# Linear attention with two MoE layers: the attention stage in a fixed order on three engines, set conversion steps, own PSUM banks, a Heron step

## The chip, the cores and the metric

The kernel runs on one core of a Trainium2 chip. The metric is the device time of one execution in microseconds (us). TensorE (PE in the profile) multiplies, VectorE (DVE) and ScalarE (ACT) work elementwise, SyncE (SP) issues the loads and stores. A kernel before and a kernel after the change compute the same function of the same inputs.

## The reference, cut to what matters

```python
batch, n_heads, seq, head_dim = (4, 8, 576, 64)          # n_tokens 2304, d_model 512
kv = np.einsum('bhsd,bhse->bhde', k, v)
out = np.einsum('bhsd,bhde->bhse', q, kv)
rms = np.sqrt(np.mean(out * out, axis=-1, keepdims=True) + 1e-06)
x = (out / rms * g_norm)                                 # then heads side by side: 2304 x 512
h = x @ w_in                                             # 512 -> 2048
g = h * np.clip(h + 3.0, 0.0, 6.0) / 6.0
x = g @ w_out                                            # 2048 -> 512
p = domain_probs / (domain_probs.sum(-1, keepdims=True) + 1e-09)
for e in range(4):                                       # 512 -> 1024 -> 512
    h = np.maximum(x @ w1[e], 0.0)
    out += p[:, e:e + 1] * (h @ w2[e])
```

`moe_w_in` and `moe_w_out` arrive as 64-bit floats, `x` and everything else as 32-bit.

## The kernel before, in words

The work has three stages: attention, the first MoE, the second MoE. The change touches the first, and the order in which the second begins.

Attention works on eight half-batches (`NHB`), each four heads of one batch. For half-batch i, `att_load` issues the loads of q, k and v on SP, 576 KB each, into seven buffers taken in turn. `att_q` transposes q on PE (`pq`, the last of nine columns into `kvp`), and ScalarE copies it to `qT`. `att_kv` adds up k transposed times v on PE (`kvp`), and ScalarE copies the blocks to `kvbd`. `att_out` multiplies qT with kvbd on PE (`po`, three PSUM banks); ScalarE squares it into `xt` and VectorE reduces the squares to `ssq`. `att_rms` makes the reciprocal root from it, in small steps on 128 x 20 elements, and scales po into `xt`. `att_x` transposes the scaled tile on PE (`px`, three pieces), ScalarE writes the high part `xh` and VectorE the low part `xl` of what the MoE reads. The loop over i runs `att_q` and `att_kv` of i, `att_out` and `att_rms` of i - 1 and `att_x` of i - 2.

The first MoE takes 16 tiles of weights (`ftiles`) in groups (`UNITS1`), and for each group goes over five blocks of tokens (four of 512, one of 256). `ff_in` is the first product of one tile and one block: 12 matmuls into a `psa` bank, then two steps on ScalarE and two on VectorE that leave `gH` and `gL`. `ff_out` is the second product, 12 matmuls into four banks, three items (`LAG`) behind `ff_in`. At a group's end `ff_end` copies (first group, ScalarE) or adds (later groups, VectorE) the banks to `acc`. Some first products (`EARLY`, `fill`) run during the attention.

Each weight tile must be turned from 64-bit to two 32-bit parts: `convert` does it in two halves, each with three steps on ScalarE and seven on VectorE, over raw data that `load_raw` brings into three buffers. `conv(k)` runs k pieces of it in the attention, `pull` runs it during the MoE by a budget per item.

The program is recorded in the order of the code; a scheduler then decides the order on each engine, and places the waits. PSUM has eight banks: two in `psa` (q transposes, first products), five in `psb` and one in `psc` (all else).

Of the kernel before, what the change touches and what calls it, by code (L numbers as in the profile page):

```python
# [17 lines left out]
def kernel(  # L18
# [34 lines left out]
    UNITS1 = (2, 4, 4, 6)  # L53
# [7 lines left out]
    NA = NW - UNITS1[0]  # L61
    LAG = 3
    FMAX = 3.0e38
# [18 lines left out]
    psb = ctx.enter_context(tc.tile_pool(name="psb", bufs=5, space=bass.MemoryType.PSUM))  # L82
    psc = ctx.enter_context(tc.tile_pool(name="psc", bufs=1, space=bass.MemoryType.PSUM))
# [3 lines left out]
    def bank_b(shape, name):  # L87
        turn[0] += 1
        pool, tag = (psc, "c") if turn[0] % 6 == 0 else (psb, "b")
        return pool.tile(shape, F32, tag=tag, name=name)  # L90
# [4 lines left out]
    three = const.tile([P, 1], F32, name="three")  # L95
    gcol = const.tile([P, 1], F32, name="gcol")
# [13 lines left out]
    raw = {}  # L110

# [18 lines left out]
    def convert(n):  # L130

        u, f = ftiles[n]
        w = wp.tile([P, 2, 2, KD * P], F32R, tag=f"w{(NA + n) % NW}", name="w")
        W[u, f] = w

        for h in range(2):
# [9 lines left out]
                out=xf, in0=xf, scalar1=2.0 ** -15, scalar2=122880.0, op0=ALU.max, op1=ALU.min)  # L146
            nc.vector.tensor_scalar(
                out=x, in0=x, scalar1=5, scalar2=2,
                op0=ALU.logical_shift_left, op1=ALU.logical_shift_right)
            yield 670  # L150
            nc.vector.scalar_tensor_tensor(
                out=a, in0=hi, scalar=0xC0000000, in1=x, op0=ALU.bitwise_and, op1=ALU.bitwise_or)
            nc.vector.tensor_scalar(out=x, in0=a, scalar1=0xFF800000, scalar2=None, op0=ALU.bitwise_and)
            yield 940
            nc.vector.tensor_tensor(out=r, in0=r, in1=xf, op=ALU.mult)
            nc.vector.tensor_tensor(out=r, in0=r, in1=a.bitcast(F32), op=ALU.add)
            yield 1200
# [3 lines left out]
            load_raw()  # L161
            yield 600


# [38 lines left out]
    def att_q(i):  # L203
# [3 lines left out]
        qv = qTs.rearrange("p r (s j) -> p r s j", j=CJ)  # L207
        pq = [psa.tile([P, CB, CP], F32, tag="a", name="pq") for _ in range(NP)]
        t["kvp"] = kvp = [bank_b([P, 2, D], "kvp") for _ in range(NP)]
        for j in range(CJ):  # L210
            for x in range(2):
                for r in range(NP):
                    to = pq[r][half[x ^ r], j, :] if j < CB else kvp[r][half[x ^ r], 1, :]
                    nc.tensor.matmul(  # L214
                        to, lhsT=t["q"][half[x], r, j, :], rhs=ident[half[x], half[x]], start=True, stop=True)
        for r in range(NP):
            nc.scalar.activation(out=qv[:, r, :, :CB], in_=pq[r].rearrange("p j s -> p s j"), func=AF.Copy)  # L217
        for r in range(NP):
            nc.scalar.activation(out=qv[:, r, :, CB], in_=kvp[r][:, 1, :], func=AF.Copy)

    def att_kv(i):
# [4 lines left out]
        for j in range(CJ):  # L226
            for x in range(2):
                for r in range(NP):
                    nc.tensor.matmul(  # L229
                        kvp[r][half[x ^ r], 0, :], lhsT=t["k"][half[x], r, j, :], rhs=t["v"][half[x], r, j, :],  # L230
                        start=(j == 0), stop=(j == CJ - 1))
        for r in range(NP):
            for x in range(2):
                nc.scalar.activation(
                    out=kvbd[i % 2][half[x ^ r], r, half[x]], in_=kvp[r][half[x ^ r], 0, :], func=AF.Copy)

    def att_out(i):
# [5 lines left out]
        for tt in banks(b):  # L243
            po = psb.tile([P, 2, NP, P], F32, tag="b", name="po")
# [14 lines left out]
    def att_rms(i):  # L259
# [4 lines left out]
        va, r0, w1_, ri = (sp.tile([P, 5, HH], F32, tag=n, name=n) for n in ("va", "r0", "nw", "ri"))  # L264

        def scale():
            for g, tt in enumerate(banks(b)):
# [22 lines left out]
    def att_x(i):  # L290
# [8 lines left out]
        def bank(rs, o0, o1):  # L299
            px = psb.tile([P, len(rs), o1 - o0], F32, tag="b", name="px")  # L300
# [18 lines left out]
        for r in range(NP):  # L319
            bank([r], *long)  # L320
        bank(list(range(NP)), *short)
# [7 lines left out]
    def ff_in(u, t, f):  # L329
# [10 lines left out]
        nc.scalar.activation(out=r, in_=ph, func=AF.Relu, bias=three[:, 0:1])  # L340
        nc.vector.scalar_tensor_tensor(out=r, in0=r, scalar=6.0, in1=ph, op0=ALU.min, op1=ALU.mult)  # L341
        nc.scalar.activation(out=gH, in_=r, func=AF.Copy)
        nc.vector.tensor_tensor(out=gL, in0=r, in1=gH.bitcast(F32), op=ALU.subtract)
        gt[u, t, f] = gH, gL

# [32 lines left out]
    EARLY = [(0, t, f) for f in range(UF[0]) for t in range(2)]  # L378
    nearly = [0]

    def fill():
        ff_in(*EARLY[nearly[0]])
        nearly[0] += 1

# [409 lines left out]
```

## Time and profile before

| what | value |
|---|---|
| median of 3 runs | 1231.76 us (1231.2 to 1231.81) |
| the profiled execution | 1232.57 us |
| its span, from the first to the last instruction | 1230.8 us |
| PE, VectorE, ScalarE busy | 1213.0, 759.0, 574.6 us |
| mean granted share of PE's clock | 0.993 |

The span is what the rows of the trace cover; the execution's time has 1.8 us more around it. Matmuls overlap, so that a busy PE may still run below its rate.

### The profile page before, as it was taken

What the parts mean: (1) busy time and instruction counts of PE and PEld (TensorE: products, weight loads), DVE (VectorE), ACT (ScalarE), POOL (GpSimd) and SP (SyncE); (2) the same over time, 40 slices, a digit from 0 to 9 for tenths busy, and PEclk for the clock granted to TensorE, in tenths of its full rate; (3) what the DMA queues carried; (4) which work ended last, traced back from release to release, by engine and by line L of the source; (5) the groups of instructions that cost most, each with busy time, mean ns of one, the idle gap of its engine ahead of it and who ended that gap; (6) DMA issues with size and microseconds to landing.
All of it is one profiled execution on the core that took longest, in us unless ns stands there. A gap on an engine that the chain in (4) does not pass through costs nothing.

```text
span 1230.8 us, 17514 instructions
## 1 busy us (share of the span) xinstructions
PE 1213.0 (99%) x7069; PEld 1067.4 (87%) x7069; DVE 759.0 (62%) x1457; ACT 574.6 (47%) x1146; POOL 1.6 (0%) x12
## 2 busy tenths in 40 slices
PE   7999999999999999999999999999999999999998
PEld 5778888888888889999999989999999899999997
DVE  6879993794533655565656576656565866565643
ACT  6667742542422434444444455444444644444442
POOL 0000000000000000000000000000000000000000
PEclk8999999999999999999999999999999999999999
DMA  9802320120010002222122222212222221112101
GB/s 359 258 22 69 104 86 1 52 69 1 26 44 1 1 1 69 69 69 69 69 69 69 69 86 103 69 69 69 69 69 69 73 98 64 66 66 66 68 34 52
DMA packets 60833, 87.15 MB, mean 71 GB/s; under 512 B 5200, under 2 KB 37968, under 8 KB 60752
## 3 DMA queue, kind: packets, MB, share of 16 engines
q1 hardware_dynamic: 60592, 86.03, 20.7%
q8 instruction: 55, 0.90, 0.3%
q14 instruction: 26, 0.21, 0.1%
q10 hardware_dynamic: 160, 0.00, 0.0%
HBM read 81.30 MB, written 4.72 MB: 70 GB/s over the span
## 4 chain that ended last, share of the span: by engine, by line
PE 94%; DVE 3%; DMA 2%; ACT 1%; issue 0%
PE po L636 30%; PE po L357 16%; PE qa L662 14%; PE qb L662 14%; PE ph L334 5%; PE ph L335 5%; PE ph L336 5%; PE po L247 1%; PE kvp L229 1%; DVE acc L652 1%; DMA qin<-in_q_dram 1%; DVE xs L550 1%; PE px L305 1%; DMA kin<-in_k_dram 1%; DVE st L609 1%; PE pq L214 0%
## 5 line engine op out<-in xcount | busy, mean ns | idle before, releaser
L636 PE MATMUL po<-wout,g 128*128 128x512 f32 x1728 | 402.0, 390 | 0.0
L636 PEld LDWEIGHTS po<-wout,g 128*128 128x128 f32 x1728 | 323.6, 188 | 65.4
L662 PE MATMUL qb<-xs,win 128*128 128x384 f32 x1008 | 203.4, 336 | 1.2 <-ACT us L702 1.2
L662 PE MATMUL qa<-xs,win 128*128 128x384 f32 x1008 | 203.2, 336 | 0.1
L357 PE MATMUL po<-gH,w 128*128 128x512 f32 (+1 forms) x640 | 193.7, 368 | 0.0
L549 ACT ACTIVATE wout<-raw 128x512 fp32r<-128x512 f32 x96 | 55.4, 624 | 275.4 <-PE po L636 275.4
L662 PEld LDWEIGHTS qb<-xs,win 128*128 128x128 f32 x1008 | 178.1, 188 | 3.8 <-ACT us L702 1.8
L662 PEld LDWEIGHTS qa<-xs,win 128*128 128x128 f32 x1008 | 178.2, 188 | 2.7 <-ACT st L698 0.4
L550 DVE TENSOR_TENSOR wout<-raw,wout 128x512 fp32r<-128x512 f32 x96 | 62.2, 689 | 159.0 <-ACT wout L549 159.0
L357 PEld LDWEIGHTS po<-gH,w 128*128 128x128 f32 x640 | 117.1, 189 | 20.1
L340 ACT ACTIVATE r<-ph,three 128x512 f32<-128x512 f32 (+1 forms) x80 | 51.4, 642 | 149.0 <-PE ph L336 149.0
L341 DVE SCALAR_TENSOR_TENSOR r<-r,ph 128x512 f32<-128x512 f32 (+1 forms) x80 | 50.6, 632 | 113.6 <-ACT r L340 113.5
L334 PE MATMUL ph<-xh,w 128*128 128x512 f32 (+1 forms) x320 | 118.5, 370 | 0.7 <-ACT qT L217 0.7
L335 PE MATMUL ph<-xl,w 128*128 128x512 f32 (+1 forms) x320 | 118.3, 370 | 0.0
L336 PE MATMUL ph<-xh,w 128*128 128x512 f32 (+1 forms) x320 | 118.0, 369 | 0.0
L357 PE MATMUL po<-gL,w 128*128 128x512 f32 (+1 forms) x320 | 117.8, 368 | 0.0
L691 DVE SCALAR_TENSOR_TENSOR g<-st,g 128x384 fp32r<-128x384 f32 x96 | 53.5, 558 | 81.2 <-ACT g L688 81.2
L688 ACT ACTIVATE g<-cs 128x384 fp32r<-128x384 f32 x96 | 49.8, 518 | 59.6 <-DVE cs L704 57.4
L691 DVE SCALAR_TENSOR_TENSOR g<-cs,g 128x384 fp32r<-128x384 f32 x96 | 53.3, 555 | 28.1 <-ACT g L688 28.1
L334 PEld LDWEIGHTS ph<-xh,w 128*128 128x128 f32 x320 | 60.4, 189 | 11.1 <-ACT qT L217 0.8
L335 PEld LDWEIGHTS ph<-xl,w 128*128 128x128 f32 x320 | 60.5, 189 | 10.0
L336 PEld LDWEIGHTS ph<-xh,w 128*128 128x128 f32 x320 | 60.3, 188 | 10.1
(95 smaller groups left out, 1248.8 us busy)
## 6 DMA issues: line engine op xcount, KB each, us to landing
raw<-in_moe_w_dram SPq DMA_DIRECT2D x96, 512.0 KB, 4.2
raw<-in_moe_w_in_dram SPq DMA_DIRECT2D x16, 512.0 KB, 3.8
raw<-in_moe_w_out_dram SPq DMA_DIRECT2D x16, 512.0 KB, 3.7
qin<-in_q_dram SPq DMA_DIRECT2D x8, 576.0 KB, 8.2
kin<-in_k_dram SPq DMA_DIRECT2D x8, 576.0 KB, 6.8
vin<-in_v_dram SPq DMA_DIRECT2D x8, 576.0 KB, 6.9
out_dram<-acc SPq DMA_DIRECT2D x18, 256.0 KB, 2.0
dp<-in_moe_domain_probs_dram SPq DMA_DIRECT2D x1, 36.0 KB, 4.7
```

Of the source, the lines that this page charges most:

```text
L334: nc.tensor.matmul(ph, lhsT=w[:, 0, c, :], rhs=xH[t][:, c, :], start=(c == 0), stop=False)
L335: nc.tensor.matmul(ph, lhsT=w[:, 0, c, :], rhs=xL[t][:, c, :], start=False, stop=False)
L336: nc.tensor.matmul(ph, lhsT=w[:, 1, c, :], rhs=xH[t][:, c, :], start=False, stop=(c == KD - 1))
L340: nc.scalar.activation(out=r, in_=ph, func=AF.Relu, bias=three[:, 0:1])
L341: nc.vector.scalar_tensor_tensor(out=r, in0=r, scalar=6.0, in1=ph, op0=ALU.min, op1=ALU.mult)
L357: nc.tensor.matmul(po_t[u, t][o], lhsT=lhsT, rhs=rhs, start=(f == 0 and m == 0), stop=(f == UF[u] - 1 and m == 2))
L549: nc.scalar.activation(out=dst[0], in_=src, func=AF.Copy)
L550: nc.vector.tensor_tensor(out=dst[1], in0=src, in1=dst[0].bitcast(F32), op=ALU.subtract)
L636: nc.tensor.matmul(ps[i], lhsT=lhsT, rhs=w[:, f, y], start=(j == 0 and f == 0 and m == 0), stop=(j == FP - 1 and f == 1 and m == 2))
L662: nc.tensor.matmul(bank, lhsT=w[:, wy, AOP[m], c], rhs=xs[m][:, xy, c], start=first and n == 0, stop=n == 5, skip_group_check=True)
L688: nc.scalar.activation(out=g[f][:, 0, t], in_=src, func=func)
L691: nc.vector.scalar_tensor_tensor(out=g[f][:, 1, t], in0=src, scalar=0.0, in1=g[f][:, 0, t].bitcast(F32), op0=ALU.max, op1=ALU.subtract)
```

## The change

The attention loop is written anew, in a block that keeps the order of the code on PE, ScalarE and VectorE. Half-batch 0 runs its q and kv ahead of the loop; turn i then has `att_out(i)`, `att_q(i + 1)`, the norm of i, `att_kv(i + 1)`, at turns 3, 5 and 7 a first product of the MoE, `att_x(i - 1)` and a set number of conversion pieces, each of a single VectorE step. `kvp` of both head pairs lies in one bank of its own, po has three banks of its own, the first piece of px one; the second and third piece of px go to the two psa banks. Three copies evacuate kvp instead of six. The six banks of the MoE's second products take the place of these when the attention has ended. The norm takes the root straight from `ssq` on ScalarE, and a Heron step on half of it: r = s + v/s, inverted, with s half the root and v a quarter of the mean. The MoE has five groups (1, 2, 3, 4, 6 tiles) instead of four (2, 4, 4, 6), and each group its own budget of conversion steps per item. Raw loads that the attention's conversions free buffers for are issued at turn 6, and the sums for `prob` are made at the end of the attention.

```diff
-    UNITS1 = (2, 4, 4, 6)
+    UNITS1 = (1, 2, 3, 4, 6)
...
+    RATE = (4200, 3000, 2600, 2900, 0)
...
-    psb = ctx.enter_context(tc.tile_pool(name="psb", bufs=5, space=bass.MemoryType.PSUM))
-    psc = ctx.enter_context(tc.tile_pool(name="psc", bufs=1, space=bass.MemoryType.PSUM))
+    attps = ExitStack()
+    psk = attps.enter_context(tc.tile_pool(name="psk", bufs=1, space=bass.MemoryType.PSUM))
+    psp = attps.enter_context(tc.tile_pool(name="psp", bufs=1, space=bass.MemoryType.PSUM))
+    psx = attps.enter_context(tc.tile_pool(name="psx", bufs=1, space=bass.MemoryType.PSUM))
...
-            load_raw()
+            if held[0] is None:
+                load_raw()
+            else:
+                held[0] += 1
...
-        for r in range(NP):
-            for x in range(2):
-                nc.scalar.activation(
-                    out=kvbd[i % 2][half[x ^ r], r, half[x]], in_=kvp[r][half[x ^ r], 0, :], func=AF.Copy)
+        kb = kvbd[i % 2].rearrange("p r (x e) -> p (r x) e", x=2)
+        nc.scalar.activation(out=kb[half[0], 0:4:3, :], in_=kvp[half[0], :, 0, :], func=AF.Copy)
+        nc.scalar.activation(out=kb[half[1], 1:3, :], in_=kvp[half[1], :, 0, :], func=AF.Copy)
+        nc.scalar.activation(out=t["qv"][:, :, :, CB], in_=kvp[:, :, 1, :], func=AF.Copy)
...
+            lambda: nc.scalar.activation(
+                out=s0, in_=ssq, func=AF.Sqrt, scale=0.25 / D, bias=eps4[:, 0:1]),
             lambda: nc.vector.tensor_scalar(
-                out=va, in0=ssq, scalar1=1.0 / D, scalar2=1e-6, op0=ALU.mult, op1=ALU.add),
-            lambda: nc.scalar.activation(out=r0, in_=va, func=AF.Sqrt),
-            lambda: nc.vector.reciprocal(out=r0, in_=r0),
+                out=va, in0=ssq, scalar1=0.25 / D, scalar2=0.25e-6, op0=ALU.mult, op1=ALU.add),
+            lambda: nc.vector.reciprocal(out=r0, in_=s0),
             lambda: nc.vector.scalar_tensor_tensor(
-                out=w1_, in0=va, scalar=FMAX, in1=r0, op0=ALU.min, op1=ALU.mult),
-            lambda: nc.vector.tensor_tensor(out=w1_, in0=w1_, in1=r0, op=ALU.mult),
-            lambda: nc.vector.tensor_scalar(
-                out=w1_, in0=w1_, scalar1=-0.5, scalar2=1.5, op0=ALU.mult, op1=ALU.add),
-            lambda: nc.vector.tensor_tensor(out=ri, in0=w1_, in1=r0, op=ALU.mult),
+                out=va, in0=va, scalar=FMAX, in1=r0, op0=ALU.min, op1=ALU.mult),
+            lambda: nc.vector.tensor_tensor(out=va, in0=va, in1=s0, op=ALU.add),
+            lambda: nc.vector.reciprocal(out=ri, in_=va),
...
-        for r in range(NP):
-            bank([r], *long)
-        bank(list(range(NP)), *short)
+        piece(psx, "x", [0], *long)
+        piece(psa, "a", [1], *long)
+        piece(psa, "a", list(range(NP)), *short)
...
-    EARLY = [(0, t, f) for f in range(UF[0]) for t in range(2)]
+    EARLY = [(0, t, 0) for t in range(NB - 1)]
...
+    FILLS = (3, 5, 7)
+    with tc.manual_schedule(engines={mybir.EngineType.PE, mybir.EngineType.Activation, mybir.EngineType.DVE}):
+        conv(9)
+        qc = att_q(0)
+        warm(4)
+        for x in qc:
             x()
+        att_kv(0)
+        conv(5)
+        for i in range(NHB + 1):
+            if i + 2 < NHB:
+                att_load(i + 2)
+            if i == NHB - 2:
+                for _ in range(held[0]):
+                    load_raw()
+                held[0] = None
+                nc.sync.dma_start(out=dp, in_=moe2_domain_probs.rearrange("(t p) e -> p t e", p=P))
+            nxt = i + 1 < NHB
+            if i < NHB:
+                att_out(i)
+                qc = att_q(i + 1) if nxt else [lambda: None] * 2
+                rms = att_rms(i)
+                qc[0]()
+                rms[0]()
+                qc[1]()
+                for x in rms[1:]:
+                    x()
+            if nxt:
+                att_kv(i + 1)
+            later = fill(True) if i in FILLS else [lambda: None] * 4
+            later[0]()
+            later[1]()
+            em = att_x(i - 1) if i else []
+            for m, (x, y) in enumerate(em):
+                x()
+                if m == 1:
+                    later[2]()
+                y()
+            later[3]()
+            conv({0: 4, 1: 1, 2: 1, 3: 3, 5: 2, 6: 1, 7: 1}.get(i, 0))
```

What that makes of the queues is shown at three places. The first is PE's queue at the start, from the q transposes of half-batch 0 (`pq` and `kvp` of `qin`) on; `po` is the output product. Before:

```order
L214 MATMUL pq<-ident,qin 64x64 x32
L214 MATMUL kvp<-ident,qin 64x64 x4
L229 MATMUL kvp<-vin,kin 64x64 x36
L214 MATMUL pq<-ident,qin 64x64 x32
L214 MATMUL kvp<-ident,qin 64x64 x4
L247 MATMUL po<-kvbd_110,qT 128x128 x5
```

Now (`zp` are matmuls on zeros that were all at the very front before):

```order
L221 MATMUL kvp<-ident,qin 64x64 x4
L221 MATMUL pq<-ident,qin 64x64 x32
L454 LDWEIGHTS zero
L454 MATMUL zp<-zero 128x512
...
L236 MATMUL kvp<-vin,kin 64x64 x36
L254 MATMUL po<-kvbd_114,qT 128x128 x8
L254 MATMUL po<-kvbd_114,qT 64x128 x2
```

po of half-batch 0 has moved ahead of the q transposes of half-batch 1. The second place is VectorE's queue in one half-batch without conversion steps, from the reductions to the scaling of `xt`; `xl` is the low part of an earlier half-batch. Before:

```order
L256 TENSOR_REDUCE ssq<-xt 128x8 x2
L256 TENSOR_REDUCE ssq<-xt 64x4
L316 SCALAR_TENSOR_TENSOR xl_120<-px,gcol,xh_115 128x384
L277 TENSOR_SCALAR va<-ssq 128x20
L316 SCALAR_TENSOR_TENSOR xl_120<-px,gcol,xh_115 128x384
L280 RECIPROCAL r_1122<-r_1122 128x20
L281 SCALAR_TENSOR_TENSOR nw<-va,r_1122 128x20
L283 TENSOR_TENSOR nw<-nw,r_1122 128x20
L316 SCALAR_TENSOR_TENSOR xl_121<-px,gcol,xh_116 128x2x192
L284 TENSOR_SCALAR nw<-nw 128x20
L286 TENSOR_TENSOR ri<-nw,r_1122 128x20
L269 TENSOR_TENSOR xt<-po,ri 128x512 x2
```

Now, for half-batch 5, a turn with a first product (line 349 is a step of it):

```order
L263 TENSOR_REDUCE ssq<-xt 128x8 x2
L263 TENSOR_REDUCE ssq<-xt 64x4
L286 TENSOR_SCALAR va<-ssq 128x20
L288 RECIPROCAL r_1056<-s_1055 128x20
L289 SCALAR_TENSOR_TENSOR va<-va,r_1056 128x20
L291 TENSOR_TENSOR va<-va,s_1055 128x20
L292 RECIPROCAL ri<-va 128x20
L276 TENSOR_TENSOR xt<-po,ri 128x512 x2
L276 TENSOR_TENSOR xt<-po,ri 64x256
L349 SCALAR_TENSOR_TENSOR r<-r,ph 128x512
L322 SCALAR_TENSOR_TENSOR xl_124<-px,gcol,xh_119 128x384 x2
L322 SCALAR_TENSOR_TENSOR xl_125<-px,gcol,xh_120 128x2x192
```

The low parts have moved from between the norm's steps to behind the scaling. The third place is VectorE's queue in half-batch 6 of the new order, where lines 148 to 162 are conversion steps that the MoE's budget calls for:

```order
L263 TENSOR_REDUCE ssq<-xt 64x4
L148 TENSOR_SCALAR x<-x 128x512
L286 TENSOR_SCALAR va<-ssq 128x20
L151 TENSOR_SCALAR x<-x 128x512
L288 RECIPROCAL r_1216<-s_1215 128x20
L155 SCALAR_TENSOR_TENSOR a<-raw,x 128x512
L289 SCALAR_TENSOR_TENSOR va<-va,r_1216 128x20
L158 TENSOR_SCALAR x<-a 128x512
L291 TENSOR_TENSOR va<-va,s_1215 128x20
L160 TENSOR_TENSOR r<-r,x 128x512
L292 RECIPROCAL ri<-va 128x20
L162 TENSOR_TENSOR r<-r,a 128x512
```

Here the scheduler has put steps that are recorded behind the block in between the block's own.

## Rows read from the trace of the kernel before

**Rows 1.** The page: PE's busy time, its 40 slices, v's loads to landing.

```profile
PE 1213.0 (99%) x7069; PEld 1067.4 (87%) x7069; DVE 759.0 (62%) x1457; ACT 574.6 (47%) x1146; POOL 1.6 (0%) x12
...
PE   7999999999999999999999999999999999999998
...
vin<-in_v_dram SPq DMA_DIRECT2D x8, 576.0 KB, 6.9
```

**Rows 2.** Three stretches: length, busy us (instructions) by engine, clock, DMA.

```profile
17.66:93.54 75.88, 70.54 (x1218) 58.96 (x1216) 60.66 (x151) 50.13 (x127) 0.00 (x0) 0.92 0.55 184
100.00:160.00 60.00, 60.00 (x289) 50.58 (x288) 57.74 (x107) 43.09 (x77) 0.00 (x0) 1.00 0.33 99
100.00:475.00 375.00, 375.00 (x1819) 317.35 (x1818) 235.76 (x415) 156.16 (x263) 0.00 (x0) 1.00 0.13 40
```

**Rows 3.** Timeline of PE, 92 to 99 us: start, us, instruction, count.

```profile
93.54 0.40 PE L357 MATMUL po<-gH,w 128*128 128x512 f32 x1
...
94.23 0.39 PE L334 MATMUL ph<-xh,w 128*128 128x512 f32 x1
...
96.96 0.39 PE L357 MATMUL po<-gH,w 128*128 128x512 f32 x1
...
97.41 0.60 PE L305 MATMUL px<-ident,xt 128*128 128x128 f32 x4
...
98.08 1.01 PE L305 MATMUL px<-ident,xt 128*128 128x128 f32 x6
```

**Rows 4.** Timeline of PE at the start.

```profile
10.91 1.39 PE L229 MATMUL kvp<-vin,kin 64*64 64x64 f32 x72 [3.34 <-ACT qT L219]
...
17.66 2.50 PE L247 MATMUL po<-kvbd,qT 128*128 128x128 f32 x10
```

**Rows 5.** Timeline of SP: the issue of v of half-batch 0.

```profile
2.27 0.47 SPq L177 DMA_DIRECT2D vin<-in_v_dram  x1
```

**Rows 6.** Timeline of ScalarE: the copies of qT of half-batch 0.

```profile
9.61 1.07 ACT L217 ACTIVATE qT<-pq 128x512 f32<-128x512 f32 x2
```

**Rows 7.** Timeline of VectorE in a later half-batch.

```profile
65.96 1.84 DVE L256 TENSOR_REDUCE ssq<-xt 128x8 f32<-128x512 f32 x3 [1.43 <-ACT xt L253]
...
68.98 0.27 DVE L280 RECIPROCAL r<-r 128x20 f32<-128x20 f32 x1
69.28 0.18 DVE L281 SCALAR_TENSOR_TENSOR nw<-va,r 128x20 f32<-128x20 f32 x1
...
71.10 1.61 DVE L269 TENSOR_TENSOR xt<-po,ri 128x512 f32<-128x512 f32 x3
```

**Rows 8.** Timeline of PE: q transposes, and po of two successive half-batches.

```profile
24.00 1.16 PE L214 MATMUL pq<-ident,qin 64*64 64x64 f32 x64
...
55.25 2.63 PE L247 MATMUL po<-kvbd,qT 128*128 128x128 f32 x20
...
64.08 2.63 PE L247 MATMUL po<-kvbd,qT 128*128 128x128 f32 x20
```

**Rows 9.** Groups of VectorE, 100 to 475 us: count, busy us, mean ns, idle before.

```profile
L373 DVE TENSOR_TENSOR acc<-po,acc 128x512 f32<-128x512 f32 (+1 forms) x56 | 34.0, 645 | 1.0 <-PE po L357 1.0
L155 DVE TENSOR_TENSOR r<-r,x 128x512 f32<-128x512 f32 x25 | 17.3, 691 | 0.9
...
L145 DVE TENSOR_SCALAR x<-x 128x512 f32<-128x512 f32 x25 | 10.6, 425 | 0.8 <-ACT x L142 0.5
```

**Rows 10.** PE's waits, 17 to 94 us: total us, times, longest.

```profile
PE px L305 <- DVE xl L316: 1.4, 4, 0.5
```

**Rows 11.** Stretches of 10 us; the third number from the end is PE's clock.

```profile
10.00:20.00 10.00, 6.29 (x154) 5.74 (x154) 6.97 (x13) 6.16 (x18) 0.00 (x0) 0.64 0.99 371
20.00:30.00 10.00, 8.35 (x238) 7.38 (x238) 9.22 (x22) 8.05 (x23) 0.00 (x0) 0.85 1.05 405
30.00:40.00 10.00, 8.79 (x174) 7.60 (x174) 9.57 (x24) 6.26 (x17) 0.00 (x0) 0.83 0.79 273
70.00:80.00 10.00, 9.34 (x115) 7.77 (x115) 4.49 (x10) 4.94 (x15) 0.00 (x0) 0.83 0.01 2
```

More of the change, by code (lines that the diff above doesn't have):

```diff
@@ L110 @@
     raw = {}
+    held = [0]
     todo = [(n, h) for n in range(len(ftiles)) for h in range(2)]
@@ L242, in att_out @@
         t["po"] = []
-        for tt in banks(b):
-            po = psb.tile([P, 2, NP, P], F32, tag="b", name="po")
+        for g, tt in enumerate(banks(b)):
+            po = psp.tile([P, 2, NP, P], F32, tag=f"p{g}", name="po")
             for m, (o, w) in enumerate(tt):
@@ L297, in att_x, with piece @@
         em = []
[L299 to L300 removed]
+        def piece(pool, tag, rs, o0, o1):
+            px = pool.tile([P, len(rs), o1 - o0], F32, tag=tag, name="px")
             for y, r in enumerate(rs):
@@ L327, with ff_in @@
     po_t = {}
-    def ff_in(u, t, f):
+    def ff_in(u, t, f, later=False):
         n = BLK[t][1]
@@ L339, in ff_in @@
         r = rp.tile([P, TB], F32, tag="r", name="r")[:, :n]
[L340 to L343, printed above, removed]
         gt[u, t, f] = gH, gL
+        parts = [
+            lambda: nc.scalar.activation(out=r, in_=ph, func=AF.Relu, bias=three[:, 0:1]),
+            lambda: nc.vector.scalar_tensor_tensor(
+                out=r, in0=r, scalar=6.0, in1=ph, op0=ALU.min, op1=ALU.mult),
+            lambda: nc.scalar.activation(out=gH, in_=r, func=AF.Copy),
+            lambda: nc.vector.tensor_tensor(out=gL, in0=r, in1=gH.bitcast(F32), op=ALU.subtract),
+        ]
+        if later:
+            return parts
+        for x in parts:
+            x()
     def ff_out(u, t, f):
@@ L376, with fill @@
     NI = len(items)
-    EARLY = [(0, t, f) for f in range(UF[0]) for t in range(2)]
+    EARLY = [(0, t, 0) for t in range(NB - 1)]
     nearly = [0]
-    def fill():
-        ff_in(*EARLY[nearly[0]])
+    def fill(later=False):
         nearly[0] += 1
+        return ff_in(*EARLY[nearly[0] - 1], later=later)
     def step(n):
@@ L392, in step @@
         if 0 <= n - LAG + 1 < NI:
-            u, t, f = items[n - LAG + 1]
-            if f < UF[u] - 1 or u == 0:
-                budget[0] = min(budget[0] + 2100, 2100)
-                pull(n)
+            rate = RATE[items[n - LAG + 1][0]]
+            budget[0] = min(budget[0] + rate, rate)
+            pull(n)
     start = {}
@@ L488 @@
+    attps.close()
+    psb = ctx.enter_context(tc.tile_pool(name="psb", bufs=1, space=bass.MemoryType.PSUM, reuse_waits="tile"))
     while nearly[0] < len(EARLY):
@@ L493 @@
         step(n)
-        if n == 8:
-            nc.vector.tensor_reduce(out=psum_e, in_=dp, axis=AX.X, op=ALU.add)
-            nc.vector.tensor_scalar(out=psum_e, in0=psum_e, scalar1=1e-9, scalar2=None, op0=ALU.add)
-            nc.vector.reciprocal(out=psum_e, in_=psum_e)
-            nc.vector.tensor_scalar(out=psum_e, in0=psum_e, scalar1=1.0 / 6.0, scalar2=None, op0=ALU.mult)
-            nc.vector.tensor_tensor(
-                out=prob, in0=dp, in1=psum_e.unsqueeze(2).to_broadcast([P, NTT, E]), op=ALU.mult)
         if n == N3:
```

89 lines of the change are left out of this document (37 added, 52 removed).

## The prediction

> **What bounds the kernel now.** I read the page first: TensorE (PE) is busy for 99% of the span, and its row of slices is below nine tenths only in the first slice and the last [rows 1]. So the whole kernel can only end earlier where PE waits or works at half clock. The table of stretches says where that is: from 100 to 475 us PE is busy for 375.00 of 375.00 us, while the stretch from 17.66 to 93.54 us, the attention, has PE busy for 70.54 of 75.88 us and VectorE for 60.66, which is 80% [rows 2]. What follows 100 us consists of the same matmuls in both kernels, so it moves as a block. A mean over the kernel hides this; the change touches some 90 us of 1231.
>
> To compare two attention stages that interleave the first MoE differently, I use one marker, A: the time from which PE has nothing but MoE work left, if all MoE work done earlier were put behind it. In the trace the first second-layer matmul (line 357) starts at 93.54 us. Four first products are behind PE by then; one takes from 94.23 to 96.96, 2.73 us. Ten of the attention's transposes are still to come (4 and 6, of which six took 1.01 us with the tail of the last), together 1.1 us [rows 3]. A = 93.54 - 4 x 2.73 + 1.1 = 83.7 us. A later or earlier A moves the end by as much, provided that PE isn't made to wait after it.
>
> **The change, part by part.**
>
> *The start.* Before, the first output product (po) starts at 17.66 us, the product of k and v of half-batch 0 at 10.91 [rows 4]; between them PE has the transposes of half-batch 1 ahead of po in its queue, and waits for q and for ScalarE, which has weight conversions ahead of its copies. In the new order po(0) stands right behind kv(0), and kv has no copy of q to wait for. v of half-batch 0 is issued at 2.27 us [rows 5] and such a load takes 6.9 us [rows 1]: 9.2 us. The product adds 1.39 [rows 4], 10.6. The two qT copies on ScalarE end at 9.61 + 1.07 = 10.7 [rows 6]; three short copies follow, for which I estimate 0.3 us each from those 0.53 us for 512 columns: po(0) at 11.6 us. The bounds are 11.2 (copies at half of that) and 17.66. The first raw weights go ahead of q as before, the third raw load now goes behind k and v of half-batch 1, so nothing that po needs gets later. Two tiny g loads move from ScalarE's queue to SP's; what they hold up there is half-batch 2, needed some 8 us later.
>
> *The chain of a half-batch.* In the old order VectorE's lower parts (xl) and conversions stand between the small steps of the norm. The three reductions of one half-batch end at 65.96 + 1.84 = 67.80 us and the scaling starts at 71.10, 3.3 us later [rows 7]. In the new order five small steps follow one another: 0.27 for a reciprocal, 0.18 for the others, 1.1 us, and about 0.1 for the root on ScalarE. The Heron step itself saves one small step and swaps another for a reciprocal: 0.1 us per half-batch. A new turn, counted from the start of po: first reduction at +1.88 (64.08 to 65.96, [rows 7, 8]), reductions done at +3.7, norm at +5.0, scaling (1.61) at +6.6, three lower parts of 0.6 at +8.4. PE in the meantime has po 2.63, 72 q transposes 1.3 (64 take 1.16), kv 1.39 and ten transposes 1.1: 6.4 us [rows 3, 4, 8]. So the next po starts at +6.4, its first reduction at +8.3, just when VectorE is free: a turn of 6.5 us, with both engines nearly full, against 8.83 between two po's of the old order (55.25 and 64.08, [rows 8]). The own po banks allow it: bank 0 is released with the first third of the scaling, at +5.7, before PE comes back.
>
> *The conversions.* Up to the first second-layer product, VectorE's queue behind po(0) holds 27 conversion steps in the new order and 30 in the old (counted in the two orders), at most 0.69 us each [rows 9]; six steps of first products against five; the sums for the domain probabilities (1 us) have moved out, and the last half-batch's scaling and lower parts, of which the old order had left some 2.4 us for later, have moved in. Net it is 60.66 - 1.7 + 0.7 - 0.8 - 1.0 + 2.4 = 60 us of VectorE: the same work. What can change is when it starts and how full VectorE is. The single conversion steps are queued at set places, but in half-batches 6 and 7 steps of later weights still stand between the steps of the norm, so there the turn is longer, not the total.
>
> *T1, the time of the first second-layer product.* Lower bound: VectorE 96% busy as from 100 to 160 us [rows 2], after the 1.88 us of the first turn: 13.5 + 60 / 0.96 = 76 us. Upper bound: the old pace, 75.88 us from po(0): 87.5. By turns: 11.6 + 1.9 + 8 x 6.5 + 33 conversion and first-product steps that add about 0.5 (0.43 to 0.69 less the overlap of neighbours) = 82. I add 2 us for waits that a queue in fixed order meets in the three half-batches with a first product, where PE's turn is 6.4 + 2.73 = 9.1 and VectorE's and PE's needs don't match: 84 us.
>
> *After T1.* Three first products are done instead of four, and no transposes are left. A' = 84 - 3 x 2.73 + w, where w is waiting in the first MoE items, between 0 and 4; I take 2. A' = 77.8, 5.9 us before the old A.
>
> *The MoE in five groups of 1, 2, 3, 4, 6.* Twenty more additions to acc at 0.65 us are 13 us of VectorE [rows 9], and the matmuls are the same. I cost this at nothing: from 100 to 160 us VectorE is already 96% busy and PE still loses nothing, 60.00 of 60.00 [rows 2], since each g is made three items before its use. If that cover went, one group's last four additions, 2.6 us, would show at each of 20 places. Of the raw loads held back, one stands on SP's queue ahead of k and v of half-batch 7 and waits for a raw buffer that a conversion step of half-batch 3 frees, some 15 us before kv(7): nothing, unless half-batch 3 comes that much later. The dp load is used only after the attention.
>
> The sum: 1232.57 - 5.9 = 1226.7 us for the profiled execution; the median of the runs is 0.8 below that execution, so **1226 us**.
>
> **The rivals.**
>
> *VectorE gets fuller (faster still).* Without waits in the half-batches T1 comes at 79 (between the bounds 76 and 82): A' = 79 - 8.2 + 2 = 72.8, 10.9 us earlier, 1221 us. For it: the turn above has no idle time. Against: in the old kernel no 10 us of attention with loads arriving showed PE undisturbed.
>
> *PE stands in its fixed order (no change).* The second and third transposed pieces now go to the two psa banks that the q transposes and the first product use too, so PE waits there for the qT copies, or for two steps of the first product, and nothing behind may pass. In the old order PE waited for such a bank four times, 1.4 us in all, 0.5 at the longest [rows 10]. If it costs 0.74 us in each of eight half-batches, the 5.9 us are gone: 1232 us. The Trainium skill (PSUM — Partial Sum Buffer, summary of rules) says to keep readers and matmuls on different banks and to guard by bank. By that rule these waits are certain, and their size is what decides.
>
> *The clock (slower).* The granted clock was 0.64, 0.85 and 0.83 in the three stretches from 10 to 40 us and 0.83 from 70 to 80 [rows 11]: at the lower of its two levels for (0.36 + 0.15 + 0.17 + 0.17) x 20 = 17 us, 21% of the attention, after stretches in which PE ran short bursts with waits between. PE's work from po(0) to T1 is 8 x 6.4 + 3 x 2.73 = 59 us at 2.4 GHz. If PE runs at 1.2 GHz for a share f of that work, T1 = 11.6 + 3 + 59 x (1 + f), which is 89.9, where A' equals the old A, at f = 0.27. With f = 0.35 T1 is 94.3 and the kernel ends 4.4 us later, 1236 us. For it: the new order keeps small bursts, and PE was busy for only 6.29 of the 10 us in which the clock first fell. Against: its start has no PE wait as long as the 3.34 us ahead of kv(0) [rows 4]. The Trainium skill (TensorE: Matmul & The Clock Gate, HAM oscillation) describes just this for bursts shorter than the waits between them: each next burst starts at half clock. By that rule the tail, where VectorE makes PE wait, falls too; the slices at 70 to 80 us agree for the old kernel.
>
> **How the numbers follow.** About 0.2%, 2.5 us, can be told from no change here. The forecast, T1 from 82 to 87.5 with w from 0 to 2, gives gains of 9.9 to 2.4: 1222 to 1229.4 us, chance 0.60. Faster still 0.14, no change 0.15, slower 0.11. So faster is 0.74, same 0.15, slower 0.11. The range leaves out the slower cases and the end of the faster one: 1219.5 to 1232.
>
> **What would show it.** Right: po(0) near 11.6 us; plain turns near 6.5 to 7.5 us; VectorE over 80% from po(0) to T1; T1 near 84 with no transposes behind it; PE at full from about 90 us to 470; the second MoE starting 6 us earlier and lasting as long. Wrong: T1 past 88; a granted clock below 0.8 after 25 us; PE idle ahead of px by more than 0.7 us in each half-batch; or, after A', PE waiting for acc additions or for weights of the second or third group, which would show as PE idle between 90 and 160 us and which I priced at nothing.

## The result, and the profile after

The kernel after takes 1243.02 us (median of five runs, 1239.93 to 1243.95) against 1231.59 for the kernel before: a ratio of 1.0089, interval 1.0078 to 1.0101. It is 11.4 us slower, outside the range of the prediction, which forecast a gain. The profiled execution has a span of 1240.6 us (1242.34 with what lies around it), against 1230.8.

The stretches of the kernel after (length, busy us and instructions of TensorE, of its weight loads, of VectorE, ScalarE and GpSimd, then TensorE's clock, the DMA share and GB/s; the first runs from the first output product of the attention to the first second-layer product):

```profile
12.95:89.53 76.58, 63.73 (x1284) 54.22 (x1285) 61.65 (x142) 49.47 (x109) 0.00 (x0) 0.91 0.56 189
...
20.00:30.00 10.00, 6.10 (x169) 5.55 (x169) 6.60 (x16) 4.28 (x11) 0.00 (x0) 0.88 0.97 369
30.00:40.00 10.00, 9.50 (x186) 8.39 (x185) 6.04 (x14) 8.14 (x18) 0.00 (x0) 0.78 0.72 232
70.00:80.00 10.00, 7.69 (x143) 6.71 (x135) 8.82 (x22) 6.89 (x16) 0.00 (x0) 0.83 0.18 54
80.00:90.00 10.00, 7.76 (x33) 5.68 (x33) 9.97 (x24) 6.15 (x13) 0.00 (x0) 0.79 0.18 52
90.00:160.00 70.00, 70.00 (x320) 57.01 (x320) 65.87 (x126) 43.20 (x79) 0.00 (x0) 0.98 0.28 83
100.00:475.00 375.00, 375.00 (x1749) 307.59 (x1748) 243.39 (x428) 148.70 (x252) 0.00 (x0) 1.00 0.12 38
```

The attention ends earlier than before: T1 is 89.53 us, where it was 93.54 [rows 3]. The loss lies behind it, where TensorE waits for nothing: from 100 to 475 us it is busy for 375.00 of 375.00 us, at full clock, as before, but gets 1749 matmuls done instead of 1819 [rows 2]. A busy share can't show this; counts can, if they are of one shape. These two are not: of the 1819, 348 have 256 columns, of the 1749 only 280, because the kernel after is further from the end of the first MoE at 475 us. From 150 to 440 us both get 192 of 256 columns done, and of 512 columns 1178 before and 1148 after, 2.5% fewer. The timeline of TensorE in that stretch shows it matmul by matmul, first the kernel before, then the kernel after:

```profile
201.37 0.39 PE L334 MATMUL ph<-xh,w 128*128 128x512 f32 x1
201.60 0.39 PE L335 MATMUL ph<-xl,w 128*128 128x512 f32 x1
...
204.09 0.39 PE L357 MATMUL po<-gH,w 128*128 128x512 f32 x1
```

```profile
200.22 0.40 PE L340 MATMUL ph<-xh,w 128*128 128x512 f32 x1
200.45 0.39 PE L341 MATMUL ph<-xl,w 128*128 128x512 f32 x1
...
203.02 0.40 PE L370 MATMUL po<-gH,w 128*128 128x512 f32 x1
```

The twelve matmuls of one first product take 204.09 - 201.37 = 2.72 us before and 2.80 after: 226.7 and 233.3 ns from start to start, of the same instruction on the same shapes. The first MoE ends, and the second starts, 7.1 us later. The second, whose code is untouched, then takes 1240.6 - 487.0 = 753.6 us where it took 1230.8 - 479.9 = 750.9, and its matmuls of 384 columns have a longer median (ns min/median/max, first and last start; before, then after):

```profile
L662 PE MATMUL qb<-xs,win x1008: 333/334/440, 479.9 to 1218.4; 128*128 128x384 f32 x168
```

```profile
L687 PE MATMUL qb<-xs,win x1008: 333/338/444, 487.0 to 1228.2; 128*128 128x384 f32 x168
```

What is not the same in the two kernels is where the operands lie. In both programs as built, every tile in SBUF starts at a multiple of 32 bytes. The Heron step brings a constant with a tile of its own,

```diff
+    eps4 = const.tile([P, 1], F32, name="eps4")
```

4 bytes that take 32, and the other small tiles keep their number. So everything behind them on the left side of SBUF moves up by 32 bytes: x and g of the first MoE, its sums acc, and xs, the tiles that the second MoE reads. x of the first block starts at byte 91136 before, a multiple of 64, and at 91168 after. The weights, on the right side, stay at multiples of 64. In each of these matmuls x, g or xs is the operand that streams through (the moving one), and the weights are the one that is loaded (the stationary one).

In the attention, the largest waits of TensorE up to 90 us (total us, times, longest) are:

```profile
PE kvp L236 <- issue: 3.9, 1, 3.9
PE po L254 <- DVE xt L276: 3.3, 3, 1.8
PE px L311 <- DVE r L349: 3.2, 3, 2.1
PE po L254 <- ACT w L164: 2.3, 1, 2.3
```

### The profile page after: what moved, and what is told of

It reads as the page before. It is cut to its first block, busy times and chain, and to the rows that moved or that the text cites. A ratio compares the mean times of both kernels' runs of the same rounds, so it can differ in the third digit from the quotient of the medians.

```text
span 1240.6 us, 17493 instructions
## 1 busy us (share of the span) xinstructions
PE 1218.1 (98%) x7068; PEld 1065.6 (86%) x7069; DVE 770.0 (62%) x1469; ACT 571.8 (46%) x1122; POOL 1.6 (0%) x13
## 4 chain that ended last, share of the span: by engine, by line
PE 93%; DVE 4%; ACT 1%; issue 1%; DMA 0%; SPq 0%; DVEq 0%
PE po L661 30%; PE po L370 16%; PE qa L687 14%; PE qb L687 14%; PE ph L340 5%; PE ph L341 5%; PE ph L342 5%; PE po L254 1%; DVE acc L677 1%; DVE xs L575 1%; DVE st L634 1%; PE pq L221 1%; DMA qin<-in_q_dram 0%; PE kvp L236 0%; PE px L311 0%
## 5 line engine op out<-in xcount | busy, mean ns | idle before, releaser
L370 PE MATMUL po<-gH,w 128*128 128x512 f32 (+1 forms) x640 | 196.7, 373 | 0.0
L349 DVE SCALAR_TENSOR_TENSOR r<-r,ph 128x512 f32<-128x512 f32 (+1 forms) x80 | 50.6, 632 | 106.9 <-ACT r L348 106.6
L340 PEld LDWEIGHTS ph<-xh,w 128*128 128x128 f32 x320 | 60.2, 188 | 12.6 <-DVE xl L322 0.4
```

The source lines that it names most:

```text
L340: nc.tensor.matmul(ph, lhsT=w[:, 0, c, :], rhs=xH[t][:, c, :], start=(c == 0), stop=False)
L349: lambda: nc.vector.scalar_tensor_tensor(out=r, in0=r, scalar=6.0, in1=ph, op0=ALU.min, op1=ALU.mult),
L370: nc.tensor.matmul(po_t[u, t][o], lhsT=lhsT, rhs=rhs, start=(f == 0 and m == 0), stop=(f == UF[u] - 1 and m == 2))
```

## The experiments

My theory was **address**: the 32 bytes cost about 12 us, and without them the change gains. Its rival was **schedule**: five groups, new waits or the attention cost the time. Beside these I wanted to know why T1 was not at 84 us. In the first three sets of runs the kernel before, measured on the same chip, took 1232.12, 1232.08 and 1231.95 us, and in the last 1232.46.

### Only the address undone, or only it done

Kernel after, left padding 40:

```diff
-    PADL, PADR = 48, 248
+    PADL, PADR = 40, 248
```

> The kernel after, with the padding on the left of SBUF cut from 48 to 40 floats, so that everything behind the small tiles goes back 32 bytes, to the places it had before. Nothing else is changed. Theory 'address': a 512-column matmul of the first MoE takes 226.7 ns from start to start again where the kernel after takes 233.3, and a 384-column matmul of the second MoE 174.6 where it takes 176.7; the time falls by about 12 us, to 1230 us (1228 to 1232), and the first second-layer product still starts near 89 us. Rival 'schedule': five groups, waits or the attention make the difference, so the pitch and the time stay, 1243 us.

Kernel before, left padding 56 (`PADL, PADR = 56, 248`):

> The kernel before, with the left padding raised from 48 to 56 floats: everything behind it moves up by 32 bytes, and no instruction changes. Theory 'address': the matmuls of the first MoE go to 233.3 ns and the 384-column ones of the second to 176.7; the time rises by about 12 us, to 1243 us (1241 to 1245). Rival 'schedule': 1231.6 us as before.

Measured: 1230.82 us for the first, ratio to before 0.9989 (0.998 to 0.9998), and 1243.03 for the second, 1.0089 (1.0076 to 1.0102), the very ratio of the change. TensorE from 100 to 475 us (busy, count, clock, DMA) of the first and of the second:

```profile
100.00:475.00 375.00, 375.00 (x1821) 1.00 0.13 42
```

```profile
100.00:475.00 375.00, 375.00 (x1752) 1.00 0.12 37
```

Eight floats of padding, which nothing reads, take the whole loss away from the kernel after and bring the same loss to the kernel before. As the cause of the loss, "schedule" has fallen. In the first kernel the second MoE starts at 477.4 us and takes 750.8 again.

### Which operand it is

Kernel before, right padding 240 (`PADL, PADR = 48, 240`), and kernel before with both shifts (`56, 240`):

> The kernel before, with the right padding cut from 248 to 240 floats: now the converted weights (stationary operand of every MoE matmul but one kind), the second MoE's g (stationary) and its output weights (moving operand) move by 32 bytes, and the first MoE's x, g and the second's xs (moving) stay. Theory 'moving operand': only the second MoE's output products become slower, 1728 of them by about 6 ns, 10 to 12 us: 1242 to 1244 us, with 226.7 ns kept in the first MoE. Theory 'stationary operand': the first MoE goes to 233.3 ns and the output products slow down too. Theory 'difference of the two': the first MoE slower, the output products unchanged, since both of their operands moved. Rival 'no address effect': 1231.6.

> The kernel before with both shifts: left padding 56 and right padding 240 floats, so that moving and stationary operands of all MoE matmuls are moved by 32 bytes together. Theory 'difference of the two': what counts is where the two operands lie to each other within 64 bytes, so the first MoE is back at 226.7 ns and the time at 1229 to 1232 us, with each shift alone having cost 5 and 11 us. Theory 'each for itself': the costs add up, 1246 to 1249 us.

Measured: 1236.69 us, 1.0041 (1.0029 to 1.0053), for the first and 1232.5, 1.0002 (0.9993 to 1.0011), for the second. TensorE from 100 to 475 us of the first and of the second:

```profile
100.00:475.00 375.00, 375.00 (x1754) 1.00 0.12 37
```

```profile
100.00:475.00 375.00, 375.00 (x1819) 1.00 0.13 40
```

So it is neither operand alone. With the places as bytes past a multiple of 64, and the mean time from one matmul's start to the next, waits left out, over the 768 second-layer products of 512 columns in the first MoE and the 2016 matmuls of 384 columns in the second:

| kernel | x, g / weights | 512 columns | xs / weights | 384 columns | median of runs |
|---|---|---|---|---|---|
| before | 0 / 0 | 227.1 ns | 0 / 0 | 174.9 ns | 1231.6 us |
| after | 32 / 0 | 233.3 | 32 / 0 | 176.8 | 1243.0 |
| after, left 40 | 0 / 0 | 227.1 | 0 / 0 | 174.8 | 1230.8 |
| before, left 56 | 32 / 0 | 233.3 | 32 / 0 | 176.9 | 1243.0 |
| before, right 240 | 0 / 32 | 233.2 | 0 / 32 | 174.0 | 1236.7 |
| before, both | 32 / 32 | 227.1 | 32 / 32 | 174.9 | 1232.5 |

For 512 columns one rule holds in all six: the two operands moved alike, 227.1 ns; 32 bytes apart, either way, 233.2 to 233.3. For 384 columns it doesn't: weights 32 bytes up made them faster, by 0.9 ns, the output products (both operands at 32) went from 227.8 to 226.7, and the second MoE took 1233.9 - 486.7 = 747.2 us. Two runs went after that. Buffers at 0, 32, 64 and 96 bytes past a multiple of 128, weights at 0:

```diff
-        gH = gp.tile([P, TB], F32R, tag="gH", name="gH")[:, :n]
+        gH = gp.tile([P, TB + 8], F32R, tag="gH", name="gH")[:, :n]
...
+            g = 0 if m in XSHOME else 8
+            xs[m] = pool.tile([P, 4 * TH + g], F32R, tag=XSHOME.get(m, f"xs{m}"), name=f"xs{m}")[
+                :, :4 * TH].rearrange("p (x c t) -> p x c t", x=2, c=2)
```

> The kernel after with padding 40, and 8 floats of room behind each buffer of g in the first MoE and behind five of the seven xs of the second, so that the four buffers of gH and of gL lie 0, 32, 64 and 96 bytes past a multiple of 128, and xs likewise, while the weights stay at 0. Theory 'mod 64': g at 0 and 64 gives 226.7 ns, at 32 and 96 233.3; xs at 0 and 64 174.7 ns, at 32 and 96 176.7. Theory 'mod 128': four different values; xs at 96 gives the 173.7 ns that the right padding of 240 showed (xs 32 bytes below its weights), at 32 176.7.

Measured, one run: 1236.32 us. g at 0, 32, 64 and 96 gave 229.3, 234.0, 231.1 and 233.6 ns; xs gave 175.8, 177.1, 173.5 and 175.8. For g, 32 and 96 are the slow ones, as "mod 64" says, but 0 and 64 are not at 227.1. A neighbour at another place isn't the reason, since the twelve products of an item all read g at one place: with g at 0 the eight that read its high part gH take 227.3 ns and the four that read its low part gL 233.1, though both parts and the weights start at a multiple of 128. So "mod 64" isn't the whole rule, and what is remains open. For xs neither theory is right: the four of the seven tiles that lie at 0 already differ by more, from 174.0 to 178.6 ns, than the four places do. And the kernel after with left 48, right 240, and xs alone moved by 96 bytes more, so that the first MoE has 32 / 32 and the second 0 / 32:

```diff
-            xs[m] = pool.tile([P, 2, 2, TH], F32R, tag=XSHOME.get(m, f"xs{m}"), name=f"xs{m}")
+            xs[m] = pool.tile([P, 4 * TH + 32], F32R, tag=XSHOME.get(m, f"xs{m}"), name=f"xs{m}")[
+                :, 24:24 + 4 * TH].rearrange("p (x c t) -> p x c t", x=2, c=2)
```

> The kernel after with its left padding of 48 as it is and the right padding at 240 floats, so that the weights lie at 32 of 128 bytes as x and g of the first MoE do, and with xs of the second MoE moved to 0 of 128, as they lay to their weights in the run with the right padding of 240. Theory 'places': the first MoE is at 226.7 ns, the 384-column matmuls of the second at 173.7 to 174.0, and the second MoE takes 747 us instead of 751: 1226 to 1228 us, ahead of both kernels and of padding 40 alone (1230.8). Rival 'that gain was not of the places': the second MoE takes 751 us as with padding 40, 1230 to 1232 us.

Measured: 1233.69 us, 1.001 (1.0001 to 1.0019). The first MoE is at 227.1 ns as expected; the 384-column matmuls take 176.0 instead of 174.0, and the second MoE 1232.6 - 479.5 = 753.1 us. A miss: the 747 us of the right padding 240 are not explained by the place of xs to its weights within 128 bytes, and stay open.

The traces hold a rival that no run takes out: the tiles on the left that ScalarE and VectorE use meanwhile, of which this run moved xs alone. The output products of the second MoE have both operands on the right, so no shift changes where these lie to each other. They stand 36 in a row. In the kernel before, ScalarE and VectorE are both busy for 71% of the time of the first twelve, and for 3% of the rest. The rest take 226.7 ns in all kernels of the table; the first twelve take 230.1 where left and right lie alike (229.9 in this last run), 227.8 to 227.9 with the left 32 bytes up and 226.8 with the right.

### The attention: a stall that no order removes

With padding 40 the change gains 1.3 us (the two profiled executions differ by 2.6); T1, the start of the first second-layer product, is 88.19 and not 84. The longest single wait is the 3.8 us of "issue" in the products of k and v of half-batch 2. Eight of its 72 products are left when TensorE stops, for 3.82 us; "issue" says that it waited for nothing that the profile shows, and k and v had landed, since 64 products had used them (timeline of TensorE, padding 40):

```profile
22.54 1.12 PE L236 MATMUL kvp<-vin,kin 64*64 64x64 f32 x63
27.48 0.49 PE L236 MATMUL kvp<-vin,kin 64*64 64x64 f32 x8 [3.82 <-issue]
...
30.20 1.22 PE L254 MATMUL po<-kvbd,qT 128*128 128x128 f32 x4
```

The page counts 55 packets of a queue of kind "instruction", 0.90 MB in all, or 16 KB each. I take it for TensorE's: 0.90 MB over its 14138 matmuls and weight loads are 64 bytes for each, and the other such queue has 0.20 MB. The DMA view of padding 40 from 19.5 to 25 us, and then from 25 to 26.2 us (packets, MB, share of 16 engines):

```profile
q1 hardware_dynamic: 1028, 2.23, 103.6%
```

```profile
q1 hardware_dynamic: 216, 0.47, 99.3%
q8 instruction: 1, 0.02, 5.0%
```

While the loads keep the DMA engines full, no block of instructions starts in these 5.5 us. By the packets of the trace one starts at 19.34 us and the next, in the stall, at 25.19; it has landed at 26.15, and at 27.48 TensorE goes on, 1.3 us later. Two runs test that reading: one without the loads of half-batches 2 to 7, which therefore leaves out part of the input, and one with four dummy matmuls more ahead of the place.

```diff
-                att_load(i + 2)
+                st[i + 2] = {x: ld[i % 2][x] for x in "qkv"}
```

> The kernel after with padding 40, without the loads of q, k and v of half-batches 2 to 7: these compute on the tiles of half-batches 0 and 1, so part of the input is left out. Theory 'instructions behind data': TensorE's stall of 3.8 us before the last eight products of k and v of half-batch 2 is a wait for its next block of instructions, whose transfer stands behind the loads (one block per 6 us while the DMA engines are full); with the loads gone the stall goes, the third and fourth output product start near 25 and 32 us instead of 30.2 and 38.2, and the first second-layer product 3 to 6 us earlier than 88.2. Rival 'clock or order': the stall stays at the same place, since no load is waited for there.

```diff
-        warm(4)
+        warm(8)
```

> The kernel after with padding 40, and eight instead of four dummy matmuls of 512 columns ahead of the first product of k and v (0.9 us more of TensorE's work at 2.4 GHz, before it waits for the copies anyway). Theory 'instructions behind data': the stall falls at a place in TensorE's instruction stream, the edge of a block; four matmuls more ahead of it move it from behind the 64th of the 72 products of half-batch 2 to behind the 60th, and it stays 3 to 4 us long. Rival 'something of that product': the stall stays behind the 64th. The time is within 0.5 us of 1230.8 by both.

Without the loads (timeline of TensorE):

```profile
25.18 0.34 PE L236 MATMUL kvp<-vin,kin 64*64 64x64 f32 x7 [0.51 <-issue]
25.45 1.36 PE L311 MATMUL px<-ident,xt 128*128 128x128 f32 x10
27.21 2.60 PE L254 MATMUL po<-kvbd,qT 128*128 128x128 f32 x20 [0.41 <-DVE xt L276]
...
33.87 0.35 PE L254 MATMUL po<-kvbd,qT 128*128 128x128 f32 x1 [0.51 <-DVE xt L276]
```

With four dummy matmuls more:

```profile
24.06 1.10 PE L236 MATMUL kvp<-vin,kin 64*64 64x64 f32 x60
28.57 0.69 PE L236 MATMUL kvp<-vin,kin 64*64 64x64 f32 x12 [3.40 <-issue]
```

Both came out as the theory said, but for two starts: without loads po(2) and po(3) were expected near 25 and 32 us and came at 27.21 and 33.87. Without loads the stall is 0.51 us, po(3) starts at 33.87 instead of 38.20, T1 is 83.88, and the time 1225.82 us, 0.9944 (0.9931 to 0.9958). The block starts at 22.82 us there, 3.7 after the one before. With four matmuls more TensorE stops four products earlier, behind the 60th, for 3.40 us, at 1230.86 us, 0.9983 (0.9974 to 0.9993). In the nine traces of this attention with its loads the blocks start 5.9 to 6.3 us apart at this place, and in these and the one without loads TensorE goes on 1.3 to 1.5 us after the block has landed. So the stall belongs to a place in TensorE's instruction stream, and to loads that fill the DMA engines at that time. The Trainium skill (Runtime: NRT & Kernel Launch, Instruction fetch mechanics) says that an engine's instructions are fetched in blocks of 16 KiB by its own queue, with the cost of crossing one mostly hidden; the blocks' size agrees with 0.90 MB in 55 packets, and the cost doesn't: here one crossing cost 3.8 us.

Two attempts to make it shorter with all loads kept: six load buffers instead of seven, and the third raw load at turn 1 instead of ahead of the loop.

```diff
-            m = natile[0] % 7
+            m = natile[0] % 6
```

> The kernel after with padding 40, and six buffers instead of seven for the loads of q, k and v: one load less is ahead, so less stands before TensorE's instruction blocks. Theory 'instructions behind data': the blocks come less than 6 us apart after 19 us, the stall in the products of half-batch 2 is shorter than 3.8 us, and the kernel is 1 to 3 us faster than with padding 40 alone. Rival: the loads come later, TensorE waits for q, k or v by name (DMA), and the time stays or grows by up to 3 us.

```diff
     att_load(1)
-    load_raw()
...
                 att_load(i + 2)
+            if i == 1:
+                load_raw()
```

> The kernel after with padding 40, and the third load of raw weights moved from before half-batch 2's loads to behind half-batch 3's. Theory 'instructions behind data': the DMA engines are full until 30 us whatever the order, so blocks still come 6 us apart and the stall stays (3 to 4 us), 1230.8 us. Rival 'this load is what stands before the block': the stall shrinks by about 1.3 us, the share of 0.5 MB at 390 GB/s, and so does the time.

Measured: 1230.17 us, 0.9981 (0.9973 to 0.999), with a stall of 4.1 us; and 1230.84 us, 0.9989 (0.998 to 0.9998), with 3.6. Neither shortened the stall beyond its scatter (3.5 to 4.0 in other runs with the loads as they were): for the first that is a miss of what I expected, and the second came out as the theory said. The 0.19% of the six buffers is the best time of a kernel that computes everything; its interval overlaps that of padding 40 alone, so that I don't call it a gain of the buffers. Other orders of the loads were not tried.

### The tail and the first products

The block of fixed order drawn over five MoE items, so that no later conversion gets between the norm steps of half-batches 6 and 7:

```diff
+    NMAN = 5
...
-    while nearly[0] < len(EARLY):
-        fill()
+        attps.close()
...
+        while nearly[0] < len(EARLY):
+            fill()
+        for n in range(NMAN):
+            step(n)
```

> The kernel after with the padding at 40, and the block of fixed order drawn over the first five MoE items as well, so that no weight conversion of these items stands between the norm steps of half-batches 6 and 7. Theory 'tail': those steps cost the tail 3 us; the first second-layer product starts at 85 to 87 us and the kernel ends 2 to 4 us before the one with padding 40 alone, 1226 to 1228 us. Rival 'work moved': VectorE has the same steps to do behind the block, TensorE waits for the second group's weights between 90 and 130 us, and the time is the same or some us longer.

No first product inside the attention:

```diff
-    FILLS = (3, 5, 7)
+    FILLS = ()
```

> The kernel after with padding 40, and no first product inside the attention: all four stand behind it. Theory 'fills cost waits': the waits ahead of the transposes for the product's step on VectorE (0.84 and 2.12 us in the last two) go away, TensorE's turns in half-batches 3, 5 and 7 are 2.7 us shorter and some more, and the first MoE ends 1 to 3 us earlier, 1228 to 1230 us. Rival 'VectorE sets the turn': without them TensorE waits for the norm instead, the products' 8 us come behind the attention in full, and the kernel ends 2 to 6 us later, 1233 to 1237 us.

The first: 1232.57 us, 1.0 (0.9991 to 1.0009), with T1 at 87.24. TensorE's clock is 0.98 from 30 to 90 us where it was 0.90 with padding 40, so the half clock of the tail is gone as well. Still the median gains nothing. The profiled execution, at 1228.95 us the fastest of the twelve, shows these waits up to 110 us, and so perhaps less than the median lost:

```profile
PE ph L341 <- DVE r L350: 3.1, 1, 3.1
...
PE ph L341 <- DVE xl L323: 1.5, 1, 1.5
```

```profile
90.00:160.00 70.00, 66.45 (x320) 55.53 (x319) 63.73 (x119) 43.91 (x80) 0.00 (x0) 1.00 0.28 83
```

TensorE loses 3.55 us from 90 to 160 us: the rival "work moved" is right, VectorE has the same steps to do behind the block. The second: 1234.49 us, 1.0018 (1.0009 to 1.0027), 3.7 more than with the first products inside. T1 is 94.81, and TensorE waits for the norm where it had first products to do:

```profile
PE po L254 <- DVE xt L276: 5.1, 3, 2.9
...
PE px L311 <- DVE xl L322: 4.2, 1, 4.2
```

"VectorE sets the turn" is right here. It is TensorE's waiting that first products fill.

## Why the prediction was wrong, point by point

**The step that failed first** is the sentence that what follows 100 us consists of the same matmuls in both kernels and so moves as a block. They are the same instructions, at other places in SBUF. From the table: 1536 matmuls of 512 columns x 6.2 ns are 9.5 us, and 384 of 256 columns became 2.9 ns faster (119.6 to 116.7), 1.1 us: 8.4 in the first MoE. In the second, 2016 x 2.0 ns are 4.0, and 1728 output products became 0.8 ns faster (227.8 to 227.1), 1.3 us: 2.7. The sum is 11.1 us, of 12.2 between the medians of the kernel after with padding 48 and 40. Between their two profiled executions it is 12.4 (spans of 1240.6 and 1228.2), and T1, 89.53 against 88.19, makes up the 1.3 that is left; whether the address moved T1 too is not shown. It stood in the diff: a new tile among the small ones, ahead of all the others, beside a padding that is nothing but a number of floats. I read the Heron step for its VectorE time, 0.1 us, and not for its place.

**T1, 84 us.** With padding 40, which takes the address out, 88.19 (its stretch from po(0) to T1, and its po(3)):

```profile
12.06:88.19 76.13, 63.36 (x1284) 53.96 (x1285) 61.67 (x142) 49.48 (x109) 0.00 (x0) 0.91 0.56 194
```

```profile
38.20 2.02 PE L254 MATMUL po<-kvbd,qT 128*128 128x128 f32 x16 [0.50 <-DVE xt L276]
```

The mis-sized term is the turn of 6.5 us in half-batch 1: po(1) to po(2) took 30.20 - 18.74 = 11.46, with the stall, half clock in the slices behind it (0.81 and 0.85 from 20 to 40 us) and TensorE's later start. Without the loads T1 is 83.88 and the kernel takes 1225.8: the forecast's own figures, in a kernel in which little delays TensorE's instructions. That they agree this closely is in part luck, since its plain turns range from 6.65 to 8.97 us. From po(3) to T1 both need 50.0 us (88.19 - 38.20, 83.88 - 33.87), so the loss lies wholly ahead of po(3). The prediction had no term for it, though the groups of the kernel before show such waits (count, busy us, mean ns, idle before and what ended it):

```profile
L247 PE MATMUL po<-kvbd,qT 128*128 128x128 f32 (+1 forms) x160 | 24.2, 304 | 1.2 <-issue 1.0 <-DVE xt L269 0.2
...
L214 PE MATMUL kvp<-ident,qin 64*64 64x64 f32 x64 | 4.8, 251 | 2.3 <-issue 1.6 <-DVE xl L316 0.5
```


**po(0), 11.6 us:** 12.95 after, 11.3 to 12.6 in the runs with padding 40 and the four dummy matmuls. **Plain turns of 6.5 to 7.5:** 6.68 and 7.48 in two of them with padding 40, 8.00 and 8.97 in two, and 11.46 in the one with the stall; with a first product 9.59 and 10.23 where 9.1 was worked out.

**The own po banks** were to keep TensorE from waiting, since the scaling releases them before it comes back. It came back earlier, three times, 3.3 us in all for xt L276. **The psa banks** (the rival of no change): TensorE waits ahead of px for a step of the first product, r L349, 3.2 us in the three half-batches that have one, and not in each of eight; the 2 us that I added for such waits were near. Of the Trainium skill's rule on sharing a bank (PSUM — Partial Sum Buffer, Summary: rules for kernel authors) the trace shows both sides: the waits came, and they don't decide.

**The clock (the rival of slower)** has the right sign and isn't the reason: the granted clock was 0.78 to 0.88 from 20 to 40 and from 70 to 90 us. That is about as in [rows 11] up to 80 us; from 80 to 90 the kernel before had 1.00. The 12.2 us go with the padding at the same clock (0.91 from po(0) to T1 in both). The prediction drew from the Trainium skill's HAM oscillation (TensorE: Matmul & The Clock Gate) that the tail falls too. It did, to 0.83 and 0.79, but not in the skill's case of bursts shorter than the waits between them: ahead of the wait of 2.3 us after which po(7) took 4.12 us instead of 2.63, TensorE had worked from 66.72 to 73.37 us without a pause.

**w, 2 us.** With padding 40 the second MoE starts 479.9 - 477.4 = 2.5 us earlier, so A' is 83.7 - 2.5 = 81.2 and w = 81.2 - (88.19 - 8.19) = 1.2. **Five groups at nothing:** right, TensorE is busy for 375.00 of 375.00 us, and at equal addresses its matmuls keep their 227.1 ns. **The conversions:** same work, 61.65 us of VectorE from po(0) to T1 against 60 forecast; keeping the conversions from between the norm steps moved T1 by 0.95 us (87.24 against 88.19), and the kernel's time gained nothing.

So the change, at equal addresses, gains what its attention gains: 1.3 us (interval 0.2 to 2.5) of the 5.9 forecast. What remains open: why the two places matter to TensorE, at what distances beyond 0 and 32 bytes they do, and what the right padding of 240 did for the second MoE.

## What to carry to other kernels

Compare the addresses of two kernels before you call an untouched stage the same, and compare the time from one matmul's start to the next, or counts of one shape, afterwards: TensorE at 100% busy and full clock was 2.7% slower here. A new small tile belongs where it moves nothing, in a free part of an old tile or behind the large ones, and padding should be set again after every change in the small tiles. A turn estimated from engine times holds only where TensorE's instructions arrive; while loads fill the DMA engines, look for waits of "issue".

## What the runs showed of the hardware

- A matmul with 512 columns of 4-byte operands took 227.1 ns from start to start in the kernels in which the tiles of its moving and its stationary operand had been moved alike, and 233.2 to 233.3 where one of the two was moved by 32 bytes, whichever it was. Matmuls of 256 columns went the other way, 119.6 to 116.7 ns with the moving operand 32 bytes up and 118.9 with the weights. With buffers at four different places in one kernel this rule didn't hold throughout.
- With the DMA engines full (103.6 and 99.3% of their time with padding 40), TensorE's next block of instructions started 5.9 to 6.3 us after the last, and TensorE stood for 3.4 to 4.1 us at the block's edge, in all nine kernels with this attention and its loads; without the loads the block came after 3.7 us and TensorE stood for 0.51. It went on 1.3 to 1.5 us after the block had landed.
